# Attention with adaLN and a mixer MLP on one core: wq resident in wo's place, K and V loaded in one stretch, one TensorE-transposed tile a head

## The chip, the cores and the metric

The kernel runs on one core of one Trainium2 chip. The metric is the device time of one execution in microseconds, as the median of the runs.

## The reference

All tensors are bf16; S = 2048 rows, D = 640, 32 heads of 128, 2048 keys a head.

```
mod = (silu(c) @ w_mod) -> sa, ca, ga, sb, cb, gb          # six vectors of 640
h = layernorm(x) * (1 + ca) + sa
q = h @ wq                       # wq: 640 x 4096, 128 columns for each head
p = softmax(q k^T / sqrt(128))   # k, v come from the caches: 32 x 2048 x 128 each
x = x + ga * ((p v, heads side by side) @ wo)               # wo: 4096 x 640
h = layernorm(x) * (1 + cb) + sb
x = x + gb * B(h)                # layernorm, w1, gelu, shifted rows, w2, residual,
                                 # layernorm, w3, gelu, w4, residual
```

## The kernel before

The program is written with a small helper that records every operation with the keys that it reads and writes, derives the waits, and issues each engine's operations in the order in which they were recorded. TensorE (PE), VectorE (DVE), ScalarE (ACT), GpSimd (POOL) and SyncE (SP) each run their own list in order. All DMAs but the ones that write the attention output are on SP's queue, `q1` in the profile; those are on GpSimd's.

There are three stages. At the start x, the modulation weights, the first heads' wq, K and V and then all of wo are loaded, x is normalized and laid out as `hT`, and head 0's Q is made. The second and longest stage is attention; the third applies wo and the MLP.

Attention walks over 512 steps `s`, 16 query tiles of 128 rows for each of 32 heads (`h, j = divmod(s, 16)`). The work for one tile:

- **QK** (line 286, TensorE): four matmuls into `Sps`, two halves of 1024 keys. It needs K of the head, transposed, in one of two buffers of `KTs`, and Q of the head in `QT`.
- **Scale and minimum** (line 559, DVE): for each half, from `Sps` into one of three buffers of `negS`, with the running minimum. POOL joins the two minima (line 569).
- **Exponential** (line 572, ACT): from `negS` into one of the eight slots of `Pb` (`ring`, `RPB = 8`).
- **Transpose of P**: into one of twelve slots of `PTs` (`RPT = 12`). Most tiles go by a DMA transpose on SP's queue (line 222), two tiles of the same pair in one issue where both are free. A tile in `PE_TILES` goes over TensorE instead: in two halves `r`, at steps `s - 3` and `s - 4`, eight 128 x 128 transposes each into one of two PSUM banks (`Oaug`, `QPp`), and each half is copied out, by ACT (line 262) or, for the second half of tile 3, by DVE (line 264).
- **P·V** (line 299, TensorE): sixteen matmuls, 11 steps behind the exponential (8 at the end); ACT copies pairs of outputs to `Of` (line 550); POOL normalizes four tiles into `On` (line 447) and writes them to a scratch tensor in HBM (line 454).

Beside this, Q of the next head is made in pieces of one matmul (line 237), twenty for each head, in the same two PSUM banks, in the half steps that the transposes leave free (`taken`, `QPIECE`), and ACT copies it out (line 244).

Loads for later heads stand in the same loop, on SP's queue between the transposes, so their place in the loop is their place in the queue: K of the next head after tile 2 (`load_k`, line 205), wq of the head after the next after tile 6 (`load_wq`, line 209, 640 rows of 256 bytes), V of the next head after tile 12 (`load_v`, line 214). The `wo` tile, 40 KB in each partition, is filled once at the start (line 335) and read only in the third stage (line 631); later w3, w4 and the output buffers lie in its place.

Of the kernel before, what the change touches and what calls it, by code (L numbers as in the profile page):

```python
# [115 lines left out]
def bass_adaLN_cond__mha_block_cached__mixer_s_mlp__prompt_kernel(  # L116
# [3 lines left out]
    _, H, SK, DH = A_k_cache.shape  # L120
    FF = B_w3.shape[1]
    assert DH == 128 and D % 128 == 0 and SQ % 512 == 0 and SK == 2048
    KT = D // 128
    NQT = SQ // 128
    NQC = SQ // 512
    NKT = SK // 128
    NFT = (FF + 127) // 128
    FL = FF - (NFT - 1) * 128
# [9 lines left out]
    with ExitStack() as es:  # L138
# [11 lines left out]
        if True:  # L150
            with ExitStack() as es1:
                sb1 = lambda name, shape, dt: es1.enter_context(nc.sbuf_tensor(name, shape, dt))
                RPB, RPT = 8, 12
                PVD, PVE = 11, 8
                PE_TILES = (3, 10)
                US = KT * (SQ + 4)
                sb1("pad", [128, 32], F32)
                ring = sb1("ring", [128, RPB + RPT, SK], BF16)
# [14 lines left out]
                o3 = o2 + 2 * KT * 128  # L173
                KTs = kv[:, 0:o1].rearrange("p (b s) -> p b s", b=2)
                Vaug = kv[:, o1:o2].rearrange("p (b k d) -> p b k d", b=2, k=NKT)
                wq = kv[:, o2:o3].rearrange("p (b k d) -> p b k d", b=2, k=KT)
                QT = kv[:, o3:o3 + 2 * SQ].rearrange("p (b q) -> p b q", b=2)
                Pb = ring[:, 0:RPB]
                PTs = ring[:, RPB:RPB + RPT].rearrange("p r (k q) -> p r k q", k=NKT)
# [23 lines left out]
                def load_k(h):  # L203
                    hb = h % 2
                    G.dma("sync", lambda e: e.dma_start_transpose(KTs[:, hb], A_k_cache[0, h]), ("k", hb), w=[("KT", hb)])

                def load_wq(h):
                    hb = h % 2
                    G.dma("sync", lambda e: e.dma_start(wq[:, hb], A_wq[:, h * 128:(h + 1) * 128].rearrange("(k p) d -> p k d", p=128)),
                          ("wq", hb), w=[("wq", hb)])  # L210

                def load_v(h):
                    hb = h % 2
                    G.dma("sync", lambda e: e.dma_start(Vaug[:, hb, :, 0:128], A_v_cache[0, h].rearrange("(t p) d -> p t d", p=128)),
                          ("v", hb), w=[("V", hb)])
# [16 lines left out]
                    return bank_of[key]  # L232

                def q_piece(h, cc, q):
                    hb = h % 2
                    jb = bank(("q", h, cc))
                    G.op("tensor", lambda t: t.matmul(JB[jb], wq[:, hb, q, :], hT[:, q, cc * 512:(cc + 1) * 512],  # L237
                                                      start=(q == 0), stop=(q == KT - 1)),
                         r=[("wq", hb), ("hT", cc, q)], w=[("J", jb)])

                def q_evac(h, cc):
                    hb = h % 2
# [20 lines left out]
                    else:  # L263
                        G.op("vector", lambda v: v.tensor_copy(dst, src), r=[("J", jb)], w=[("PT", g % RPT, r)])

                by_dve = lambda g, r: r == 1 and g % NQT == PE_TILES[0]

                taken = [u for j in PE_TILES for u in range(2 * (j + 3), 2 * (j + 5))]
                QPIECE = {}
                u = 0  # L270
                for cc in range(NQC):
# [53 lines left out]
                load_mod(0, wmod, 0, 2 * D)  # L325
                for cc in range(2, NQC):
                    load_x(cc)
                load_wq(0)
                load_k(0)
                load_v(0)  # L330
                load_mod(1, wmodr, 2 * D, 6 * D)
                if H > 1:
                    load_wq(1)
                    load_k(1)
                G.dma("sync", lambda e: e.dma_start(wo[:], A_wo.rearrange("(h p) n -> p h n", p=128)), "wo", w=["wo"])

                G.op("gpsimd", lambda g: g.memset(ident[:], 0.0), w=["id0"])
                G.op("gpsimd", lambda g: g.memset(ones_f, 1.0), w=["onesf"])
# [106 lines left out]
                def norm(gr, z):  # L445
# [5 lines left out]
                    if z < 3:  # L451
# [33 lines left out]
                vet = sm[:, 336:336 + 3 * NQT].rearrange("p (l t) -> p l t", l=3)  # L485
                mhalf = sm[:, 384:385]
                NEG = [("negS", i) for i in range(3)]
                KVK = ([("KT", b) for b in range(2)] + [("V", b) for b in range(2)] + [("wq", b) for b in range(2)]
                       + [("QT", b, cc) for b in range(2) for cc in range(NQC)])
                HTK = [("hT", cc, k) for cc in range(NQC) for k in range(KT)]  # L490
                ONK = [("On", b, z) for b in range(2) for z in range(4)]
# [24 lines left out]
                for s in range(at[-1] + LAG + 1):  # L516
# [10 lines left out]
                    for half in range(2):  # L527
                        if s < NG:
                            qk(s, half)
                        for g_ in pvs:  # L530
                            if len(pvs) == 1:
                                pv(g_, half)
                            elif g_ == pvs[half]:
                                pv(g_, 0)
                                pv(g_, 1)
                        if s == 0 and half == 1:
                            q_head0(NQC - 1)
                        if h + 1 < H and 2 * j + half in QPIECE:
                            cc, q = QPIECE[2 * j + half]
                            q_piece(h + 1, cc, q)  # L540
                            if q == KT - 1:
                                evacs.append((q_evac, h + 1, cc))
                        for r in range(2):
                            g = s - 3 - r
                            if 0 <= g < NG and is_pe(g):
                                t_piece(g, r, half)
                                if half == 1:
                                    evacs.append((t_evac, g, r))
# [19 lines left out]
                    if s < NG:  # L568
                        G.op("gpsimd", lambda g, r8=r8: g.tensor_scalar(  # L569
                            out=nm[:, r8:r8 + 1], in0=nm0[:, r8:r8 + 1], scalar1=nm1[:, r8:r8 + 1], scalar2=None, op0=ALU.min),  # L570
                            r=[("nmh", 0, r8), ("nmh", 1, r8)], w=[("nm", r8)])
                        G.op("scalar", lambda a, s=s, r8=r8: a.activation(  # L572
                            Pb[:, s % RPB, :], negS[:, s % 3, :], ACT.Exp, bias=nm[:, r8:r8 + 1], scale=-1.0),
                            r=[("negS", s % 3), ("nm", r8)], w=[("Pb", s % RPB)])
                        if not is_pe(s):
                            if s % 2 == 1 and not is_pe(s - 1):
                                transpose(s - 1, 2)
                            elif s % 2 == 1 or is_pe(s + 1):
                                transpose(s, 1)
                        if j == 2 and h >= 1 and h + 1 < H:  # L580
                            load_k(h + 1)
                        if j == 6 and h + 2 < H:
                            load_wq(h + 2)
                        if j == PVD + 1 and h + 1 < H:
                            load_v(h + 1)
                    for g_ in NORMS.get(s, []):
                        gr, z = divmod(g_, 4)
                        if z == 0:
# [35 lines left out]
                def a_pe(j):  # L624
                    b = ybank()
                    pr, z = divmod(j, 2)

                    def f(t):
                        for c0, cw in NC2:
                            for hh in range(H):  # L630
                                ins = t.matmul(YB[b][:, c0:c0 + cw], OTj[pr % 2][:, 2 * hh + z, :], wo[:, hh, c0:c0 + cw],  # L631
                                               start=(hh == 0), stop=(hh == H - 1))
                        return ins
                    G.op("tensor", f, r=[("OT", pr % 2), "wo"], w=[("S", b)])
                    return b

                def a_s1(j, b):
# [35 lines left out]
                for i in range(NQT + 1):  # L673
# [12 lines left out]
                    if 2 <= i:  # L686
                        nrm_of(1, i - 2)
                w3s = B_w3.rearrange("(k p) n -> p k n", p=128)
                G.dma("sync", lambda e: e.dma_start(w3, w3s), "w3", w=["w3", "wo"])
                G.dma("sync", lambda e: e.dma_start(w4[:, 0:NFT - 1, :], B_w4[0:(NFT - 1) * 128, :].rearrange("(f p) n -> p f n", p=128)),  # L690
                      "w4", w=["w4", "wo"])
                G.dma("sync", lambda e: e.dma_start(w4[0:FL, NFT - 1, :], B_w4[(NFT - 1) * 128:FF, :]), "w4b", w=["w4b", "wo"])
                DEL = [1, -1, 2, -2]
                segs = []
                for n in range(KT):
# [67 lines left out]
                def e_op(j):  # L763
                    b = ybank()
                    g = (j // 4) % 2
                    u = j % 2
                    q0 = (j % 4) * 128

                    def f(t):
                        for c0, cw in NC2:  # L770
                            for f_ in range(NFT):
                                ins = t.matmul(YB[b][:, c0:c0 + cw], gT[g][0:fsz[f_], f_, q0:q0 + 128], w4[0:fsz[f_], f_, c0:c0 + cw],  # L772
                                               start=(f_ == 0), stop=(f_ == NFT - 1))
                        return ins
                    G.op("tensor", f, r=["w4", "w4b", ("gT", g)], w=[("S", b)])
                    G.op("vector", lambda v: v.tensor_add(out=tmp[:, u], in0=YB[b][:, 0:D], in1=xb[:, j]),  # L776
                         r=[("S", b), ("xb", j)], w=[("tmp", u)])
                    G.op("vector", lambda v: v.tensor_mul(out=tmp[:, u], in0=tmp[:, u], in1=mod_bc[:, 3 * D:4 * D]),
                         r=[("tmp", u), "mod"], w=[("tmp", u)])
                    G.op("vector", lambda v: v.tensor_add(out=ob[:, u], in0=tmp[:, u], in1=xt[:, j]),  # L780
                         r=[("tmp", u), ("x1", j)], w=[("ob", u)] + (["wo"] if j < 2 else []))
                    G.dma("sync", lambda e: e.dma_start(out2d[j * 128:(j + 1) * 128, :], ob[:, u]), ("out", u), r=[("ob", u)], w=[("o", j)])

                for n in range(KT):
# [59 lines left out]
```

## Time and profile before

| | us |
|---|---|
| median of 3 runs | 1612.16 (1607.38 to 1612.76) |
| the profiled execution | 1604.1 |
| its span, from the first to the last instruction | 1602.3 |
| first exponential of head 0 starts | 39.1 |
| first exponential of head 1 | 81.0 |
| first exponential of head 31 | 1216.2 |
| last exponential starts | 1251.9 |

How to read the profile: the page gives each engine's busy time in the span, a row of tenths over 40 slices, the DMA queues, the chain that ended last, and the costliest groups of instructions by source line. A group's row has its count, then the busy time in all and the mean ns of one, then the idle time of its engine just before it and what ended that. The table by windows gives for a stretch of the span the busy us of PE, PEld (TensorE's weight loads), DVE, ACT and POOL with their instructions in brackets, then the granted TensorE clock, the share of time of the sixteen DMA engines (packets overlap, so it can be over 1) and GB/s. The view of waits has, for each pair of a waiting line and what it waited for, the us in all, the number of times and the longest.

### The profile page before, as it was taken

How to read it: one execution, taken by the hardware profiler on the slowest of the kernel's cores; microseconds unless marked ns; L12 is line 12 of the kernel's file. 1: busy time of each engine (PE TensorE's matmuls, PEld its weight loads, DVE VectorE, ACT ScalarE, POOL GpSimd, SP SyncE). 2: the span in 40 equal slices, each digit the busy share in tenths (PEclk: the TensorE clock that was granted, in tenths of full speed). 3: DMA queues.
4: the chain of work that ended last, by engine and by line, in shares of the span. 5: the costliest groups of instructions: out<-in, count | busy, mean ns of one | idle time of the engine just before them, and what ended most of it. 6: DMA issues, size and time to landing. Idle time of an engine off the chain costs nothing.

```text
span 1602.3 us, 34804 instructions
## 1 busy us (share of the span) xinstructions
PE 1492.6 (93%) x13978; PEld 963.0 (60%) x14231; DVE 1392.5 (87%) x2460; ACT 1288.2 (80%) x1145; POOL 622.8 (39%) x1394
## 2 busy tenths in 40 slices
PE   5799999999999999999999999999999799999998
PEld 3466666666666666666666666666666555545444
DVE  6999999999999999999999999999999266666424
ACT  4999999999999999999999999999999300055330
POOL 0144444444444444444444444444444423322000
PEclk9999999999999999999999999999999899999999
DMA  9999999999999999999999999999999994530000
GB/s 305 229 230 239 238 243 237 253 241 240 237 237 233 239 237 237 239 239 247 243 250 246 250 239 235 246 228 239 236 244 244 241 196 106 106 111 1 17 17 34
DMA packets 1167730, 333.62 MB, mean 208 GB/s; under 512 B 1148304, under 2 KB 1161552, under 8 KB 1167568
## 3 DMA queue, kind: packets, MB, share of 16 engines
q1 hardware_dynamic: 1161424, 314.59, 98.3%
q0 software_dynamic: 6144, 16.79, 3.3%
q8 instruction: 112, 1.84, 0.5%
q14 instruction: 50, 0.41, 0.1%
HBM read 43.48 MB, written 19.40 MB: 39 GB/s over the span
## 4 chain that ended last, share of the span: by engine, by line
DVE 30%; ACT 24%; PE 20%; DMA 15%; issue 10%; POOL 0%; SPq 0%; ACTq 0%; DVEq 0%
DVE negS L559 27%; ACT ring L572 19%; DMA ring<-ring 13%; PE Sps L631 8%; PE Sps L772 4%; PE Oaug L756 2%; PE QPp L756 2%; ACT ring L262 2%; ACT Of L550 2%; PE Sps L741 1%; ACT kv L244 1%; DMA ring<-in_A_x_dram 1%; DVE ring L364 1%; DMA negS<-o_scratch 1%; PE Sps L286 1%
## 5 line engine op out<-in xcount | busy, mean ns | idle before, releaser
L559 DVE TENSOR_SCALAR_CACHE_REDUCE negS<-Sps 128x1024 f32<-128x1024 f32 x1024 | 1177.2, 1220 | 22.2 <-PE Sps L286 12.5
L572 ACT ACTIVATE ring<-negS,small 128x2048 bf16<-128x2048 f32 x512 | 1011.4, 2029 | 21.9 <-DMA ring<-ring 15.7
L299 PEld LDWEIGHTS PTp<-kv,ring 128*128 128x128 bf16 x8192 | 560.0, 98 | 245.0 <-DMA ring<-ring 6.7
L286 PE MATMUL Sps<-kv 128*128 128x512 bf16 x1949 | 596.3, 383 | 62.8 <-DVE negS L559 42.9
L299 PE MATMUL PTp<-kv,ring 128*128 128x129 bf16 x8192 | 645.6, 221 | 6.5 <-DMA ring<-ring 5.6
L569 POOL TENSOR_SCALAR small<-small 128x1 f32<-128x1 f32 x512 | 145.8, 285 | 621.5 <-DVE negS L559 621.4
L286 PEld LDWEIGHTS Sps<-kv 128*128 128x128 bf16 x2048 | 124.5, 97 | 187.2 <-DVE negS L559 158.0
L447 POOL TENSOR_SCALAR On<-Of,small 128x128 bf16<-128x128 f32 x512 | 189.8, 371 | 13.0
L669 ACT COPY kv<-PTp 128x640 bf16<-128x640 bf16 x32 | 22.0, 692 | 155.0 <-PE PTp L666 154.9
L440 POOL TENSOR_TENSOR small<-Of,small 128x4 f32<-128x4 f32 x128 | 133.2, 1040 | 6.3 <-ACT Of L550 6.2
L454 POOL DMA_DIRECT2D o_scratch<-On x128 | 103.1, 806 | 40.8 <-POOL On L447 37.2
L237 PE MATMUL Oaug<-hTx,kv 128*128 128x512 bf16 x265 | 101.2, 387 | 7.9 <-ACT ring L262 4.2
L550 ACT COPY Of<-PTp 128x259 f32<-128x259 f32 x256 | 99.5, 389 | 10.5 <-PE PTp L299 10.5
L237 PE MATMUL QPp<-hTx,kv 128*128 128x512 bf16 x259 | 97.5, 381 | 2.5 <-ACT hTx L391 1.8
L559 DVE DVE_READ_ACCUMULATOR negS<-Sps 128x1 f32 x1024 | 85.4, 83 | 0.0
L612 POOL TENSOR_SCALAR On<-On 128x1 f32<-128x1 f32 x48 | 24.3, 507 | 152.9 <-DVE On L621 152.9
L639 DVE TENSOR_TENSOR ring<-Sps,mod_bc 128x640 f32<-128x640 f32 x16 | 13.2, 825 | 77.0 <-PE Sps L631 77.0
L631 PE MATMUL Sps<-wo,hTx 128*128 128x128 bf16 (+1 forms) x504 | 71.8, 304 | 5.0 <-DMA hTx<-o_scratch 4.7
L776 DVE TENSOR_TENSOR ring<-Sps,ring 128x640 f32<-128x640 f32 x16 | 13.2, 825 | 66.2 <-PE Sps L772 66.2
L631 PE MATMUL Sps<-wo,negS 128*128 128x128 bf16 (+1 forms) x504 | 69.1, 298 | 1.3 <-DMA negS<-o_scratch 0.9
L262 ACT COPY ring<-Oaug 128x1024 bf16<-128x1024 bf16 x64 | 66.2, 1034 | 0.0
L631 PEld LDWEIGHTS Sps<-wo,hTx 128*128 128x128 bf16 x512 | 40.2, 99 | 36.9 <-DMA hTx<-o_scratch 4.5
(82 smaller groups left out, 1011.2 us busy)
## 6 DMA issues: line engine op xcount, KB each, us to landing
kv<-in_A_v_cache_dram SPq DMA_DIRECT2D x32, 512.0 KB, 5.2
o_scratch<-On POOLq DMA_DIRECT2D x128, 128.0 KB, 4.5
ring<-in_A_x_dram SPq DMA_DIRECT2D x8, 640.0 KB, 4.9
kv<-in_A_wq_dram SPq DMA_DIRECT2D x32, 160.0 KB, 3.6
wo<-in_A_wo_dram SPq DMA_DIRECT2D x1, 5120.0 KB, 16.4
ring<-ring SPq DMA_TRANSPOSE x256, 7.1
ring<-in_w_mod_dram SPq DMA_DIRECT2D x1, 3200.0 KB, 13.6
out_dram<-wo SPq DMA_DIRECT2D x16, 160.0 KB, 1.8
```

The costliest lines, as they stand in the source:

```text
L237: G.op("tensor", lambda t: t.matmul(JB[jb], wq[:, hb, q, :], hT[:, q, cc * 512:(cc + 1) * 512], start=(q == 0), stop=(q == KT - 1)), r=[(" ...
L262: G.op("scalar", lambda a: a.copy(dst, src), r=[("J", jb)], w=[("PT", g % RPT, r)])
L286: ins = t.matmul(Sps[:, col:col + 512], QT[:, hb, j * 128:(j + 1) * 128], KTs[:, hb, col:col + 512], start=True, stop=True)
L299: ins = t.matmul(ob[:, 0:129], PTs[:, b, kt, :], Vaug[:, hb, kt, 0:129], start=(kt == 0), stop=(kt == NKT - 1))
L440: G.op("gpsimd", lambda g: g.tensor_tensor(out=rl[:, 4 * b:4 * b + 4], in0=Of[:].rearrange("p a z d -> p (a z) d")[:, 4 * b:4 * b + 4, 128 ...
L447: G.op("gpsimd", lambda g: g.tensor_scalar(out=On[:, b, z, :], in0=Of[:, 2 * b + z // 2, z % 2, 0:128], scalar1=rl[:, 4 * b + z:4 * b + z ...
L454: G.dma("gpsimd", lambda e: e.dma_start(o_scr[jj // 2:jj // 2 + 2, :, hh].rearrange("a p z d -> p a (z d)"), On[:, b].rearrange("p (a z) d ...
L550: G.op("scalar", lambda a, p=p: a.copy(Of[:, p % 4].rearrange("p z d -> p (z d)")[:, 0:259], PO[:, (p % 2) * 512:(p % 2) * 512 + 259]), r= ...
L559: G.op("vector", lambda v, half=half, s=s, r8=r8: v.tensor_scalar(out=negS[:, s % 3, half * 1024:(half + 1) * 1024], in0=Sps[:, half * 102 ...
L569: G.op("gpsimd", lambda g, r8=r8: g.tensor_scalar(out=nm[:, r8:r8 + 1], in0=nm0[:, r8:r8 + 1], scalar1=nm1[:, r8:r8 + 1], scalar2=None, op ...
L572: G.op("scalar", lambda a, s=s, r8=r8: a.activation(Pb[:, s % RPB, :], negS[:, s % 3, :], ACT.Exp, bias=nm[:, r8:r8 + 1], scale=-1.0), r=[ ...
L631: ins = t.matmul(YB[b][:, c0:c0 + cw], OTj[pr % 2][:, 2 * hh + z, :], wo[:, hh, c0:c0 + cw], start=(hh == 0), stop=(hh == H - 1))
```

## The change

- `wq` is no longer loaded head by head into two buffers. It lies whole in the `wo` tile, in eight groups of four heads (`WG = 4`, view `wqg`), all loaded at the start: head 0, then heads 1 to 3, then seven groups of four, 640 rows of 1024 bytes each.
- `wo` is loaded in eight blocks of four heads (512 rows of 1280 bytes), each when the Q of its four heads has been made: after tile 11 of heads 3, 7, ..., 31.
- K and V of the next head are loaded together after tile 11, in this order, followed in every fourth head by the block of wo. V had its place one tile later, K nine tiles earlier.
- `PE_TILES` is tile 11 alone, with a lag of four steps instead of three: its halves are transposed at steps 15 and 16, the second one within the next head. Both are copied out by ACT. Tiles 3 and 10 go by DMA: 3 in a pair with 2, 10 alone.
- Q's pieces move to the half steps 2 to 21 of a head.

```diff
-                PE_TILES = (3, 10)
+                PE_TILES = (11,)
+                PE_LAG = {10: 3, 11: 4}
+                WG = 4
...
-                wq = kv[:, o2:o3].rearrange("p (b k d) -> p b k d", b=2, k=KT)
+                wqg = wo[:].rearrange("p (g h) n -> p g (h n)", h=WG).rearrange("p g (k c) -> p g k c", k=KT)
...
-                def load_wq(h):
-                    hb = h % 2
-                    G.dma("sync", lambda e: e.dma_start(wq[:, hb], A_wq[:, h * 128:(h + 1) * 128].rearrange("(k p) d -> p k d", p=128)),
-                          ("wq", hb), w=[("wq", hb)])
+                def load_wq(h0, h1):
+                    g, c0 = divmod(h0, WG)
+                    G.dma("sync", lambda e: e.dma_start(
+                        wqg[:, g, :, c0 * 128:(c0 + h1 - h0) * 128],
+                        A_wq[:, h0 * 128:h1 * 128].rearrange("(k p) d -> p k d", p=128)),
+                        ("wq", h0), w=[("wq", h) for h in range(h0, h1)])
+
+                def load_wo(g):
+                    G.dma("sync", lambda e: e.dma_start(
+                        wo[:, g * WG:(g + 1) * WG, :],
+                        A_wo[g * WG * 128:(g + 1) * WG * 128, :].rearrange("(h p) n -> p h n", p=128)),
+                        ("wo", g), w=[("wo", g)] + [("wq", h) for h in range(g * WG, (g + 1) * WG)])
...
-                by_dve = lambda g, r: r == 1 and g % NQT == PE_TILES[0]
-
-                taken = [u for j in PE_TILES for u in range(2 * (j + 3), 2 * (j + 5))]
+                by_dve = lambda g, r: False
+
+                taken = [u % (2 * NQT) for j in PE_TILES for u in range(2 * (j + PE_LAG[j]), 2 * (j + PE_LAG[j] + 2))]
...
-                load_wq(0)
+                load_wq(0, 1)
                 load_k(0)
                 load_v(0)
                 load_mod(1, wmodr, 2 * D, 6 * D)
-                if H > 1:
-                    load_wq(1)
-                    load_k(1)
-                G.dma("sync", lambda e: e.dma_start(wo[:], A_wo.rearrange("(h p) n -> p h n", p=128)), "wo", w=["wo"])
+                load_wq(1, WG)
+                load_k(1)
+                for g in range(1, H // WG):
+                    load_wq(g * WG, (g + 1) * WG)
...
-                        for r in range(2):
-                            g = s - 3 - r
-                            if 0 <= g < NG and is_pe(g):
+                        for r, pt in [(r, pt) for r in range(2) for pt in PE_TILES]:
+                            g = s - PE_LAG[pt] - r
+                            if 0 <= g < NG and g % NQT == pt:
                                 t_piece(g, r, half)
...
-                        if j == 2 and h >= 1 and h + 1 < H:
-                            load_k(h + 1)
-                        if j == 6 and h + 2 < H:
-                            load_wq(h + 2)
-                        if j == PVD + 1 and h + 1 < H:
-                            load_v(h + 1)
+                        if j == PVD:
+                            if 1 <= h < H - 1:
+                                load_k(h + 1)
+                            if h < H - 1:
+                                load_v(h + 1)
+                            if h % WG == WG - 1:
+                                load_wo(h // WG)
```

The rest of the diff renames keys: Q's pieces read `wqg`, and what waited for `wo` now waits for its eight blocks.

More of the change, by code (lines that the diff above doesn't have):

```diff
@@ L205, in load_k @@
                     G.dma("sync", lambda e: e.dma_start_transpose(KTs[:, hb], A_k_cache[0, h]), ("k", hb), w=[("KT", hb)])
-                def load_wq(h):
-                    hb = h % 2
-                    G.dma("sync", lambda e: e.dma_start(wq[:, hb], A_wq[:, h * 128:(h + 1) * 128].rearrange("(k p) d -> p k d", p=128)),
-                          ("wq", hb), w=[("wq", hb)])
+                def load_wq(h0, h1):
[9 more added lines that the diff above has]
+                        ("wo", g), w=[("wo", g)] + [("wq", h) for h in range(g * WG, (g + 1) * WG)])
+                WOK = [("wo", g) for g in range(H // WG)]
                 def load_v(h):
@@ L234, in q_piece @@
                 def q_piece(h, cc, q):
-                    hb = h % 2
                     jb = bank(("q", h, cc))
-                    G.op("tensor", lambda t: t.matmul(JB[jb], wq[:, hb, q, :], hT[:, q, cc * 512:(cc + 1) * 512],
+                    G.op("tensor", lambda t: t.matmul(JB[jb], wqg[:, h // WG, q, (h % WG) * 128:(h % WG + 1) * 128], hT[:, q, cc * 512:(cc + 1) * 512],
                                                       start=(q == 0), stop=(q == KT - 1)),
-                         r=[("wq", hb), ("hT", cc, q)], w=[("J", jb)])
+                         r=[("wq", h), ("hT", cc, q)], w=[("J", jb)])
                 def q_evac(h, cc):
@@ L487, in bass_adaLN_cond__mha_block_cached__mixer_s_mlp__prompt_kernel @@
                 NEG = [("negS", i) for i in range(3)]
-                KVK = ([("KT", b) for b in range(2)] + [("V", b) for b in range(2)] + [("wq", b) for b in range(2)]
+                KVK = ([("KT", b) for b in range(2)] + [("V", b) for b in range(2)]
                        + [("QT", b, cc) for b in range(2) for cc in range(NQC)])
@@ L633, in f @@
                         return ins
-                    G.op("tensor", f, r=[("OT", pr % 2), "wo"], w=[("S", b)])
+                    G.op("tensor", f, r=[("OT", pr % 2)] + WOK, w=[("S", b)])
                     return b
@@ L688, in bass_adaLN_cond__mha_block_cached__mixer_s_mlp__prompt_kernel @@
                 w3s = B_w3.rearrange("(k p) n -> p k n", p=128)
-                G.dma("sync", lambda e: e.dma_start(w3, w3s), "w3", w=["w3", "wo"])
+                G.dma("sync", lambda e: e.dma_start(w3, w3s), "w3", w=["w3"] + WOK)
                 G.dma("sync", lambda e: e.dma_start(w4[:, 0:NFT - 1, :], B_w4[0:(NFT - 1) * 128, :].rearrange("(f p) n -> p f n", p=128)),
-                      "w4", w=["w4", "wo"])
-                G.dma("sync", lambda e: e.dma_start(w4[0:FL, NFT - 1, :], B_w4[(NFT - 1) * 128:FF, :]), "w4b", w=["w4b", "wo"])
+                      "w4", w=["w4"] + WOK)
+                G.dma("sync", lambda e: e.dma_start(w4[0:FL, NFT - 1, :], B_w4[(NFT - 1) * 128:FF, :]), "w4b", w=["w4b"] + WOK)
                 DEL = [1, -1, 2, -2]
@@ L780, in e_op @@
                     G.op("vector", lambda v: v.tensor_add(out=ob[:, u], in0=tmp[:, u], in1=xt[:, j]),
-                         r=[("tmp", u), ("x1", j)], w=[("ob", u)] + (["wo"] if j < 2 else []))
+                         r=[("tmp", u), ("x1", j)], w=[("ob", u)] + (WOK if j < 2 else []))
                     G.dma("sync", lambda e: e.dma_start(out2d[j * 128:(j + 1) * 128, :], ob[:, u]), ("out", u), r=[("ob", u)], w=[("o", j)])
```

## The prediction

> **What bounds the kernel now.** I read the page first. Parts 1 and 2 show a softmax stage that fills three quarters of the span, with every engine row and the DMA row at 9 from about 80 to 1250 us; part 3 shows one queue taking nearly all DMA time; part 5 names the two heaviest lines. Nothing there says which of DVE, ACT and DMA is the limit.
>
> ```profile
> PE 1492.6 (93%) x13978; PEld 963.0 (60%) x14231; DVE 1392.5 (87%) x2460; ACT 1288.2 (80%) x1145; POOL 622.8 (39%) x1394
> ...
> DMA  9999999999999999999999999999999994530000
> ...
> q1 hardware_dynamic: 1161424, 314.59, 98.3%
> q8 instruction: 112, 1.84, 0.5%
> ...
> L559 DVE TENSOR_SCALAR_CACHE_REDUCE negS<-Sps 128x1024 f32<-128x1024 f32 x1024 | 1177.2, 1220 | 22.2 <-PE Sps L286 12.5
> L572 ACT ACTIVATE ring<-negS,small 128x2048 bf16<-128x2048 f32 x512 | 1011.4, 2029 | 21.9 <-DMA ring<-ring 15.7
> ```
>
> So I cut the stage into heads (the table by windows). An early head takes 37.2 us, and DVE and ACT are both busy for all of it; a later one takes 37.5 to 39.6, with the same work in it and idle time beside it. The DMA rate is the same in all of them.
>
> ```profile
> 118.30:155.50 37.20, 35.73 (x366) 24.22 (x372) 37.20 (x66) 37.20 (x33) 17.44 (x40) 1.00 1.23 240
> 192.70:229.90 37.20, 35.80 (x368) 24.21 (x372) 37.20 (x66) 37.20 (x32) 17.44 (x40) 1.00 1.25 241
> ...
> 493.20:532.40 39.20, 36.51 (x371) 24.65 (x375) 37.63 (x66) 37.45 (x32) 17.46 (x40) 1.00 1.24 231
> 532.40:571.00 38.60, 35.48 (x364) 24.32 (x369) 36.99 (x66) 37.30 (x32) 17.43 (x40) 1.00 1.23 242
> ```
>
> The waits in 416 to 611 us name what ends the idle time, which the stretch 81 to 378 does not have at all: the exponential waits for a transpose to free its slot in the ring of eight.
>
> ```profile
> PE Sps L286 <- DVE negS L559: 8.5, 20, 1.4
> ACT ring L572 <- DMA ring<-ring: 7.1, 11, 1.2
> ...
> DVE negS L559 <- ACT ring L572: 3.6, 6, 1.5
> ```
>
> To see where that comes from I put the 256 transposes of line 222, in order, beside the exponentials that they need. From the end of the second exponential of tiles 0 and 1 to the landing of their transpose it is 6.2 us in head 0, then 8.9, 9.6, 10.3, 11.6, 12.7, 13.0 in heads 1 to 6, 16.1 in head 12, and 12 to 17 in all heads from 7 to 30. The backlog grows by about 1 us a head while the engines run at 37.2, then stands against the ring's limit. **The DMA queue is the bound from head 1 on**: it needs about 38.0 us a head, and the engines merely run ahead of it by eight tiles. (SyncE's waits are no evidence against it: the view books them under ACT operations, L550 and L244 among them, that no transpose needs.) Between 416 and 611 us packets were under way with next to none starting (a stall) for 29 us, and there was nothing to do for 2 us.
>
> **Prices on the queue.** In a backlogged queue the time from one landing to the next is a service time. Means in 420 to 1200 us, per head: a pair of tiles 3.52 us with no instruction fetch and no write of On in it; a single tile 1.95 to 2.08; K 2.24; V 2.72; wq 0.96 (0.81 without fetches); the pair behind wq 3.93, which is 0.41 more than the plain pair; a write of On adds about 0.9 to the pair that it meets. Each 16 KB packet of q8 is followed by a stall of 0.8 to 1.9 us; PE's instructions (13978 + 14231, 64 bytes each, make 1.81 MB of the 1.84) cause them, 2.9 a head. All twelve intervals of a head add up to 38.0.
>
> **The change, part by part, for one head.**
>
> Removed from DVE: the copy L264. From ACT: one of three L262.
>
> ```profile
> L264 DVE COPY ring<-QPp 128x1024 bf16<-128x1024 bf16 x8 | 5.5, 685 | 0.0
> ```
>
> From its start to the next start the DVE copy is 0.60 us, an ACT copy 0.90 (neighbours overlap by 0.08 and 0.13). DVE then needs 37.22 - 0.60 = 36.62, ACT 37.22 - 0.90 = 36.32. Neither is worth anything while DMA needs more. TensorE loses 16 of its 32 transposes, about 1 us at 8 in 0.8 us; it waits for DVE (L286 above), so that is worth nothing.
>
> Added to DMA: tile 3 and tile 10 join, tile 11 leaves, so 15 tiles instead of 14, still in eight issues (seven pairs and a single for six pairs and two singles). A tile is half of 3.52, +1.76; a single that becomes a pair gives 3.52 - 2.0 = +1.5, a lone single +2.0. I take 1.76, as the tile is moved by the same packets at the same rate as in a pair.
>
> wq leaves the stage: -0.81, and the -0.41 behind it, together -1.2 (ends -0.6, the median interval alone, and -1.4). It is loaded whole at the start in place of wo, 5.24 MB for 5.24 MB, in front of the first transposes as before: nothing. wo comes in eight blocks: at the start all of it took 14.35 us, from K's landing at 32.87 to its own at 47.22; a block is 1.79, per head +0.45 (up to 0.6 with an entry of its own). It is needed only in the next stage; the last block comes in head 31, which loads no K and V.
>
> PE's program shrinks from 744 to 712 instructions a head: 0.125 fetches fewer at some 1.4 us, -0.17.
>
> K and V side by side: the count of switches between transposes and copies around V is the same, and the pair behind V costs no more than one behind a transpose when each holds a write of On (4.27 against 4.44). I put 0.
>
> Sum: 1.76 - 1.2 + 0.45 - 0.17 = **+0.84 us a head, 38.85**. Ends: 1.5 - 1.4 + 0.45 - 0.25 = +0.3 and 2.0 - 0.6 + 0.6 = +2.0. DVE's 36.62 stays below all of these.
>
> The Trainium skill, VectorE: DVE Perf Modes, Rules for kernel authors, speaks against this part: transpose 128×128 on TensorE if PSUM will do as the destination, else by DMA. Advanced Engine Details and Errata, X-Bar Transpose, speaks for it: 350 to 400 GB/s expected, some 90% of a copy. The pair's 1.05 MB in 3.52 us are 298 GB/s here; at the Trainium skill's rate a tile would be an estimated 1.31 to 1.50, and the sum +0.4 to +0.6.
>
> **The moved wait.** K of the next head was issued at tile 2, with fourteen tiles to spare. Now it stands behind the transpose of tile 10 and is needed at tile 16. In the trace the first QK of the next head starts 7.6 us after the exponential of tile 10 ends (6.1 to 7.9 over the heads). K's service is 2.2 us, so the transposes may lag by 5.4 us at most, where 12 are usual. QK is behind the wait, and on TensorE behind it P·V and the second half of tile 11's transposes; DVE runs dry. Since the queue goes on working meanwhile (V, tiles 12/13 and 14/15: 2.7 + 4.3 + 3.8 = 10.8 us, before tiles 0/1 are ready about 8 to 9 us after K lands) the stall is not added to 38.85; it is how the queue's time now shows. What is lost is the head start: tiles 0/1 of the last head will lag by some 7.2 us (10.8 + 4.5 of their own, less 8) where they lagged by 12.9, so the engines end 5.7 us later against the same queue; head 31, free of K and V, gives back 1.8 (33.8 us from its second exponential to its last, against fourteen tiles at 36.62/16).
>
> **Total.** 31 heads x 0.84 = 26, + 5.7 - 1.8 = +30 on the profiled execution: 1604.1 (span 1602.3) becomes 1634. The tail behind the last head is untouched. The median of the runs stands 8 above the profiled time, so **1642**. With the two ends: +13 and +66.
>
> **The rivals.**
>
> *The queue is relieved, not loaded* (faster). If the small wq reads with 256-byte rows cost the transposes around them more than their own interval, or if a tile more in the stream costs less than half a pair, the queue may need less than DVE. For it: 29 us of stalls in 195 are not bytes, and something may be saved there. Against it: the stalls follow the fetches, which stay, and pairs without fetches run evenly at 3.5. Below 36.62 DVE decides: heads 1 to 31 start at 80.4 + 30 x 36.62 = 1179 instead of 1216, and head 31 gains 1: -38, a median of 1574. It is faster than before from -0.13 a head (31 x 0.13 = 3.9), which needs 1 us a head that I have not found. 0.21, most of it between 1580 and 1607.
>
> The Trainium skill, DMA: Bandwidth & Descriptors, Specifications, asks for 512 bytes a transfer for line rate, a rule for this rival. wq's 0.16 MB in 0.81 us are 202 GB/s against wo's 365, so the trace agrees, and that is in the -1.2.
>
> *K's wait starves the queue.* An empty queue takes about 2 us to start (head 0's pairs land 5.5 to 6.0 after the exponential, for a service of 3.5), and 10.8 of work against 8 to 9 plus 2 is a margin of nothing. If the queue stands idle for 1 us at each head, another 31: a median of 1673. For it: QK cannot start without K, and no buffer is left in between. Against it: in most heads a fetch or a write of On stretches those 10.8. 0.15.
>
> *Nothing measurable.* +0.0 a head leaves +4. 0.05.
>
> **How the numbers follow.** The forecast, slower on the queue, 0.59; its own range is 1620 to 1664. What a measurement of this kernel can tell is about 0.3%, 5 us. Faster 0.21, same 0.05, slower 0.59 + 0.15 = 0.74. The range goes from 1592, which leaves out about 0.12 of the faster rival's mass, to 1680, which leaves out 0.06.
>
> **What would show it.** Heads of 38.5 to 39.3 us; DVE at 36.6 busy in each; no copy at L264's place; 15 tiles' packets on q1. At each head's start TensorE and DVE idle together for 1 to 3 us, ended by the DMA kv<-in_A_k_cache_dram, and the exponential's waits for ring<-ring gone; transposes lag by 5 to 9 us, not 14. A lag that stays at 4 to 6 with heads of 36.6 would make the prediction wrong and the first rival right; idle slots in the DMA row at each head's start would mean the second.

## The result and the profile after

The changed kernel takes 1697.03 us (median of 4 runs, 1688.76 to 1702.4) against 1612.46; the ratio is 1.0525, with a 95% interval of 1.0475 to 1.0576. It is slower by about 85 us, where the forecast was slower by 30, and it lies above the stated range.

The page of the kernel after, with the lines that answer to those of before: a DMA row that is still at 9 through the stage, less work on DVE and ACT, more on q1.

```profile
PE 1505.5 (89%) x13474; PEld 968.5 (57%) x13719; DVE 1376.4 (81%) x2428; ACT 1282.6 (76%) x1113; POOL 622.8 (37%) x1394
...
DMA  9999999999999999999999999999999995620000
...
q1 hardware_dynamic: 1211984, 331.36, 97.7%
...
L570 DVE TENSOR_SCALAR_CACHE_REDUCE negS<-Sps 128x1024 f32<-128x1024 f32 x1024 | 1177.8, 1220 | 132.2 <-PE Sps L297 129.9
L583 ACT ACTIVATE ring<-negS,small 128x2048 bf16<-128x2048 f32 x512 | 1021.2, 2005 | 37.5 <-POOL small L580 35.0
L297 PE MATMUL Sps<-kv 128*128 128x512 bf16 x1962 | 611.9, 391 | 148.8 <-DMA kv<-in_A_k_cache_dram 101.1
```

The last row holds the news: QK (line 297 now) sat 101 us waiting for K. Before, most of its idle time was ended by DVE, as its row there says:

```profile
L286 PE MATMUL Sps<-kv 128*128 128x512 bf16 x1949 | 596.3, 383 | 62.8 <-DVE negS L559 42.9
```

The DVE row of the kernel after shows 130 us passed on, and the exponential's idle time is no longer ended by the ring.

The table by windows, heads 11 to 14 of the kernel after: DVE works for 36.3 to 37.2 us in each, but a head lasts 37.9 to 44.3. The clock column moves too: it falls with the length of the head.

```profile
487.30:525.20 37.90, 35.77 (x355) 24.20 (x361) 37.23 (x65) 37.00 (x31) 17.72 (x41) 1.00 1.17 245
525.20:569.50 44.30, 35.75 (x350) 24.25 (x354) 36.28 (x65) 36.88 (x31) 17.11 (x40) 0.92 1.22 229
569.50:609.50 40.00, 36.80 (x350) 25.06 (x356) 36.85 (x65) 37.24 (x32) 17.76 (x41) 0.96 1.20 245
609.50:647.60 38.10, 35.17 (x351) 23.88 (x357) 36.73 (x65) 37.07 (x31) 17.10 (x40) 1.00 1.20 238
```

One head's boundary in order of time. A QK pair takes 0.60 us in the first row; the next head's first QK starts 4.57 us after TensorE's last work, when K lands, and takes 1.04; DVE stands idle behind it, and behind DVE the exponential.

```profile
678.15 0.60 PE L297 MATMUL Sps<-kv 128*128 128x512 bf16 x2
...
685.16 1.04 PE L297 MATMUL Sps<-kv 128*128 128x512 bf16 x2 [4.57 <-DMA kv<-in_A_k_cache_dram]
...
686.24 1.23 DVE L570 TENSOR_SCALAR_CACHE_REDUCE negS<-Sps 128x1024 f32<-128x1024 f32 x1 [4.71 <-PE Sps L297]
```

From the start of head 1 to that of head 31 a head takes 37.84 us before and 40.97 after (1135.2 and 1229.2 us over 30).

### The profile page after: what moved, and what is told of

The parts are those of the page before. It is cut to its first block, busy times and chain, and to the rows that moved or that the text cites. A ratio compares the mean times of both kernels' runs of the same rounds, so it can differ in the third digit from the quotient of the medians.

```text
span 1697.2 us, 33782 instructions
## 1 busy us (share of the span) xinstructions
PE 1505.5 (89%) x13474; PEld 968.5 (57%) x13719; DVE 1376.4 (81%) x2428; ACT 1282.6 (76%) x1113; POOL 622.8 (37%) x1394
## 4 chain that ended last, share of the span: by engine, by line
DVE 48%; PE 24%; DMA 11%; issue 8%; ACT 7%; SPq 2%; POOL 1%; POOLq 0%
DVE negS L570 47%; DMA kv<-in_A_k_cache_dram 8%; PE Sps L643 7%; ACT ring L583 5%; PE Sps L784 4%; PE Sps L297 3%; PE PTp L310 2%; PE Oaug L768 2%; PE QPp L768 2%; SPq L234 2%; PE Sps L753 1%; PE QPp L264 1%; DMA ring<-in_A_x_dram 1%; DVE ring L375 1%; DMA negS<-o_scratch 1%
## 5 line engine op out<-in xcount | busy, mean ns | idle before, releaser
L570 DVE TENSOR_SCALAR_CACHE_REDUCE negS<-Sps 128x1024 f32<-128x1024 f32 x1024 | 1177.8, 1220 | 132.2 <-PE Sps L297 129.9
L297 PE MATMUL Sps<-kv 128*128 128x512 bf16 x1962 | 611.9, 391 | 148.8 <-DMA kv<-in_A_k_cache_dram 101.1
L310 PEld LDWEIGHTS PTp<-kv,ring 128*128 128x128 bf16 x8192 | 574.3, 100 | 256.5 <-issue 22.5
L310 PE MATMUL PTp<-kv,ring 128*128 128x129 bf16 x8192 | 661.3, 224 | 6.0 <-DMA ring<-ring 4.7
L297 PEld LDWEIGHTS Sps<-kv 128*128 128x128 bf16 x2048 | 146.3, 99 | 274.9 <-DVE negS L570 131.7
L561 ACT COPY Of<-PTp 128x259 f32<-128x259 f32 x256 | 92.3, 360 | 95.1 <-PE PTp L310 95.0
L465 POOL DMA_DIRECT2D o_scratch<-On x128 | 103.1, 806 | 40.8 <-POOL On L458 37.2
L248 PE MATMUL Oaug<-hTx,wo 128*128 128x512 bf16 x258 | 98.0, 385 | 2.9 <-DVE hTx L407 2.9
L248 PE MATMUL QPp<-hTx,wo 128*128 128x512 bf16 x260 | 98.1, 382 | 2.8 <-ACT hTx L402 2.3
L643 PEld LDWEIGHTS Sps<-wo,hTx 128*128 128x128 bf16 x512 | 40.0, 99 | 37.2 <-DMA hTx<-o_scratch 5.4
L643 PEld LDWEIGHTS Sps<-wo,negS 128*128 128x128 bf16 x512 | 39.5, 98 | 30.9 <-DMA negS<-o_scratch 0.6
```

Source lines behind the costliest of these rows:

```text
L248: G.op("tensor", lambda t: t.matmul(JB[jb], wqg[:, h // WG, q, (h % WG) * 128:(h % WG + 1) * 128], hT[:, q, cc * 512:(cc + 1) * 512], star ...
L297: ins = t.matmul(Sps[:, col:col + 512], QT[:, hb, j * 128:(j + 1) * 128], KTs[:, hb, col:col + 512], start=True, stop=True)
L310: ins = t.matmul(ob[:, 0:129], PTs[:, b, kt, :], Vaug[:, hb, kt, 0:129], start=(kt == 0), stop=(kt == NKT - 1))
L465: G.dma("gpsimd", lambda e: e.dma_start(o_scr[jj // 2:jj // 2 + 2, :, hh].rearrange("a p z d -> p a (z d)"), On[:, b].rearrange("p (a z) d ...
L561: G.op("scalar", lambda a, p=p: a.copy(Of[:, p % 4].rearrange("p z d -> p (z d)")[:, 0:259], PO[:, (p % 2) * 512:(p % 2) * 512 + 259]), r= ...
L570: G.op("vector", lambda v, half=half, s=s, r8=r8: v.tensor_scalar(out=negS[:, s % 3, half * 1024:(half + 1) * 1024], in0=Sps[:, half * 102 ...
```

## The experiments

Theory A: K's late place costs the time. Theory B: the queue is loaded more than the sum said, and K's wait is where it shows. The ratios are against the kernel before; a stretch named heads 1 to 30 goes from the first exponential of head 1 to that of head 31.

**k_back and k_late: K's place, undone and done alone.**

```diff
 # k_back, from the kernel after
-                        if j == PVD:
-                            if 1 <= h < H - 1:
-                                load_k(h + 1)
+                        if j == 2 and 1 <= h < H - 1:
+                            load_k(h + 1)
...
 # k_late, from the kernel before
-                        if j == 2 and h >= 1 and h + 1 < H:
-                            load_k(h + 1)
...
-                        if j == PVD + 1 and h + 1 < H:
+                        if j == PVD and h >= 1 and h + 1 < H:
+                            load_k(h + 1)
+                        if j == PVD and h + 1 < H:
                             load_v(h + 1)
```

> The changed kernel with one thing undone: K of the next head is again issued after tile 2 (V and the blocks of wo stay after tile 11). Theory A (K's late place starves the queue and lets TensorE's clock fall): the 101 us that QK waited for K vanish, the granted clock is 0.99 again, heads take the queue's own 38.9 us, and the time is about 1642 us (1620 to 1660), as the sum of the prediction had it without the wait. Theory B (the fifteenth tile and the blocks of wo load the queue far more than was summed, K's wait only shows it): heads stay at 40 to 41 us, limited by the ring of eight, time 1675 or more.

Measured: 1682.96 us, ratio 1.041 (1.0381 to 1.0439). QK's wait for K is gone, the clock is 0.989, and most of the lost time is still lost. In the waits of its heads 1 to 30 another line has taken K's place, the one that bounded the kernel before:

```profile
ACT ring L583 <- DMA ring<-ring: 108.2, 76, 5.6
DVE negS L570 <- ACT ring L583: 85.2, 74, 5.0
```

Heads take 40.30 us. From head 2 on the transposes lag by 11 to 22 us, 15 in the median, which is again the ring's limit. So theory B holds for most of the loss: the queue needs 40.3 us a head, not 38.85.

> The kernel before with one thing done: K and V of the next head are issued together after tile 11; wq by head, wo whole, tiles 3 and 10 on TensorE as before. Theory A: QK waits for K at each head, 2 to 3 us in the mean, with the clock falling in some; heads of 39.5 to 41 us, time 1655 to 1700. Theory B: the queue needs its 38.0 us as before and the wait replaces the ring's; time 1610 to 1630.

Measured: 1666.98 us, ratio 1.0307 (1.0276 to 1.0339), heads of 39.93 us, QK waiting for K 66 us in 29 waits, lags of mostly 6 to 9 us. Theory A is right too: with the queue's old load, K's place (and V's, one tile earlier) costs 50 us. Here the queue runs dry: over heads 1 to 30 no packet of q1 was under way for 2.33 us a head, against 1.01 in the kernel before, and half of this time lies ahead of the transpose of tiles 4 and 5. That is 1.3 of the 2.1 us by which a head is longer; how much of the rest is TensorE's clock, granted at half for 68 us in this run, was not tested. The two costs do not add (1.041 and 1.0307 alone, 1.0525 together): the kernel after waits for K and no longer for the ring. On top of the fuller queue K's place costs 1.0525 - 1.041, some 18 us, or 14 by the two medians.

**tile11 and t11_skip: the fifteenth tile.** tile11 is the kernel before with `PE_TILES = (11,)`, its lag and both copies by ACT, and nothing else. t11_skip is tile11 with the transpose of tile 3 left out from head 1 on.

```diff
 # t11_skip, from tile11
+                            if j == 3 and h >= 1:
+                                transpose(s - 1, 1)
-                            if s % 2 == 1 and not is_pe(s - 1):
+                            elif s % 2 == 1 and not is_pe(s - 1):
                                 transpose(s - 1, 2)
```

> The kernel before with one thing done: TensorE transposes tile 11 alone, all others go by DMA; K after tile 2, wq by head after tile 6, V after tile 12. By the prediction's prices +1.5 to +2.0 us a head on the queue, less 0.17 for fetches: heads of 39.4 to 39.8, time 1655 to 1670. Theory B (a tile costs the queue more than its pair's half): 1680 or more. Were DVE and ACT the bound, 0.6 us a head less: 1592.

Measured: 1680.48 us, ratio 1.0385 (1.0352 to 1.0419), heads of 40.31 us. Its wait is the ring's:

```profile
ACT ring L573 <- DMA ring<-ring: 102.9, 94, 3.8
```

> The kernel with tile 11 alone on TensorE (K after tile 2, wq by head), with the DMA transpose of tile 3 left out from head 1 on, so that 14 tiles are moved as before the change; P V of that tile works on old data. If a tile costs the queue about 2.4 us when it is backlogged: heads of 37.9, time about 1606. If a tile costs 1.76 and the rest of the 64 us comes from TensorE's new schedule or from ACT's copies: 1625 or more.

Measured: 1611.2 us, ratio 0.998 (0.9954 to 1.0006), heads of 38.13. One tile less on the queue takes back 69 us: 1680.5 - 1611.2 over 31 heads is 2.2 us a tile. It lies between the two figures of the expectation, 2.4 and 1.76, nearer to the first. All the rest of that edit (TensorE's 16 transposes fewer, DVE's copy, ACT's copy, the new half steps) is worth -0.2%, within the interval of nothing.

**wq_resident, wo_left_out, wo_by_8: the weights.** wq_resident is the kernel after with the old tiles on TensorE, K after tile 2, V and the blocks of wo after tile 12.

> The kernel before with one thing done: wq lies in wo's place and wo follows in eight blocks; K after tile 2, V after tile 12, tiles 3 and 10 on TensorE. By the prediction's prices the queue needs 38.0 - 1.2 + 0.45 = 37.25 us a head, which is where DVE and ACT stand (37.22): about 18 us faster, 1594. If the small wq reads cost no more than their median interval of 0.59, the queue needs 37.9 and the time is 1609. Theory B, with blocks of wo that cost more than 1.8 us each: 1612 or more.

Measured: 1615.19 us, ratio 0.999 (0.9968 to 1.0012): nothing.

```diff
 # wo_left_out, from wq_resident
-                        if j == PVD + 1 and h % WG == WG - 1:
+                        if j == PVD + 1 and h == H - 1:
                             load_wo(h // WG)
```

> The kernel before with wq resident in wo's place and only the last block of wo loaded (heads 0 to 27 are then multiplied with what lies there, the columns of wq); K after tile 2, V after tile 12, tiles 3 and 10 on TensorE. If the blocks are what uses up the gain of the wq loads: the queue needs 38.0 - 0.85 = 37.2 us a head and meets DVE and ACT at 37.2; about 18 us below wq_resident, 1597. If the wq loads had been free: 1612 to 1616.

Measured: 1592.72 us, ratio 0.9845 (0.9803 to 0.9887), heads of 37.36. Taking wq's loads out is worth the expected time, and seven blocks of wo eat it: 0.999 - 0.9845 is 23 us, 3.3 us a block. That is a lower bound, since wo_left_out is no longer held by the queue: its exponentials wait for the ring 4.0 us in the whole run, against 24.0 in wq_resident. The landings of wq_resident agree, with 3.6 us a block in the mean of seven. In the packets of a block the first and the last are some 4.2 us apart in most blocks (1.7 at best, in the kernel after), with the rate rising and falling between them. In all eight blocks of wq_resident the first packets of the next transpose start before the block's last, so the price is not a wait of the next entry for that last packet; what it is made of was not separated.

> The kernel before with wq resident in wo's place and wo following in four blocks of eight heads (1.31 MB) instead of eight of four; K after tile 2, V after tile 12, tiles 3 and 10 on TensorE. If a block's price is a fixed part (its packets start and end staggered over the sixteen engines, and the next transpose waits for the last) plus 1.8 us per four heads at the start's rate: a block of eight takes 5.3 instead of twice 3.5, about 7 us less in all, 1605 to 1610 against 1615. If it is paid by the byte at half the start's rate: 7 us each, 1615.

Measured: 1614.92 us, ratio 0.9981 (0.9957 to 1.0005). The landing interval of a block of eight heads was 4.5 us in the mean (three blocks), as if the price were mostly fixed; the time is that of wq_resident (0.9981 against 0.999), and a gain of 7 us is about what the two intervals could still hide. Whether the price is fixed or goes by the byte stays open.

**k_back_skip2: the same program with room on the queue.**

```diff
 # from k_back
+                            if j == 3 and h >= 1:
+                                pass
-                            if s % 2 == 1 and not is_pe(s - 1):
+                            elif s % 2 == 1 and not is_pe(s - 1):
                                 transpose(s - 1, 2)
```

> The changed kernel with K after tile 2 again, and the DMA transposes of tiles 2 and 3 left out from head 1 on (13 tiles a head; P V of these works on old data). Queue theory: with room on the queue DVE is the bound at 36.6 us a head, lags fall to 4 to 8 us, time about 1576 to 1582. If something else than the queue held the heads at 40.3, more than 1600.

Measured: 1566.87 us, ratio 0.9702 (0.9673 to 0.9732). The table by windows over heads 1 to 30 of k_back and of this kernel: DVE, third of the engines, is busy for all of the second, 36.64 us a head, as summed. The time is below the 1576 to 1582 expected, and the transposes lag by 8 to 13 us where 4 to 8 was expected.

```profile
80.80:1289.90 1209.10, 1072.73 (x10500) 706.26 (x10694) 1110.50 (x1923) 1095.50 (x901) 523.85 (x1202) 0.99 1.21 238
```
```profile
80.80:1179.90 1099.10, 1061.48 (x10492) 697.64 (x10685) 1099.10 (x1921) 1092.90 (x901) 523.24 (x1200) 1.00 1.21 234
```

The change does make DVE faster; the queue keeps it from showing.

**warm: TensorE kept busy while it waits for K.** In the kernel after, the granted clock fell to half at 19 of the 30 boundaries, in TensorE's idle time or just behind it, for 3.4 or 6.8 us and once for 10.2. These are the 18 boundaries with 2.8 us of idle time and more, and one with 2.0; at the eleven others, of 1.0 to 2.3, the clock stayed. It is 102 us in all, 25 of them in the idle time itself. In k_late it fell at every boundary with 2.4 us and more, and at six of the eight with 2.0 to 2.3. The Trainium skill, TensorE: Matmul & The Clock Gate, What's actually happening, says that the clock is halved after an idle window of about 3.4 us; the traces agree in the lengths of 3.4 us and its multiples, and show shorter idle times that did it.

```diff
 # from the kernel after
+                        if half == 0 and j == 0 and 2 <= h < H:
+                            warm()   # 28 x matmul(PO[:, 262:512], ident, hT[:, 0, 0:250])
                         if s < NG:
                             qk(s, half)
```

> The changed kernel, with 28 extra matmuls (250 columns each, into unused PSUM columns, result not used) on TensorE ahead of the first QK of heads 2 to 31, about 3 us of work in the time in which TensorE waits for K. Clock theory: in the changed kernel the heads whose wait is over 2.5 us lose another 1 to 2 us because TensorE runs at half clock after it; with the idle time filled, the clock is 0.99, heads that waited briefly lose about 1 us, the others gain; time 1670 to 1690 against 1697, and half clock under 30 us instead of 102. Rival (the clock costs nothing, the queue sets the head in any case): 1697 to 1710.

Measured: 1702.63 us, ratio 1.0526 (1.0478 to 1.0574). Half clock fell to 27 us and TensorE's idle wait for K to 48, but DVE's wait for QK is about what it was in the kernel after (129.9 us):

```profile
DVE negS L579 <- PE Sps L297: 136.2, 44, 7.4
```

The rival's figure was met. About 16 us of delay that the filler adds in the eleven short waits (3.15 us a head in its row, against 1.7 in the mean) may hide a gain of that size, so the clock's own cost is not shown to be nothing; by this working some 16 of the 85 us lost can be the clock's. The queue pauses less in this run, too: no packet of q1 was under way for 1.00 us a head, against 1.54 in the kernel after and 1.06 in k_back, and yet a head takes 41.12 us.

**third_tile and third_tile_by_2: the other way.**

```diff
 # from the kernel before
-                PE_TILES = (3, 10)
+                PE_TILES = (2, 4, 11)
-                is_pe = lambda g: g % NQT in PE_TILES
+                is_pe = lambda g: g % NQT in (2, 11) or (g % NQT == 4 and (g // NQT) % 3 == 1)
-                by_dve = lambda g, r: r == 1 and g % NQT == PE_TILES[0]
+                by_dve = lambda g, r: r == 1 and g % NQT < 11
```

> The kernel before with more on TensorE instead of less: tiles 2 and 11 in every head, and tile 4 in every third head (second halves of 2 and 4 copied by DVE). The queue gives up a third of a tile a head, 2.4 / 3 = 0.8 us, from 38.0 to 37.2; ACT rises by 0.3 to 37.5, DVE by 0.2 to 37.4. If the queue is the bound of the kernel before: heads of 37.5, about 10 to 15 us faster, 1600 to 1606. If DVE and ACT bound it: 1620 to 1625.

Measured: 1602.01 us, ratio 0.9915 (0.9887 to 0.9943), heads of 37.73.

> As third_tile, with tile 4 on TensorE in every second head: the queue gives up 1.1 us a head, ACT rises by 0.45 to 37.67 and DVE by 0.3 to 37.52. ACT is then the bound: heads of 37.7, no better than third_tile, 1600 to 1606; lags of the transposes fall to 6 to 10 us. If the queue still bound third_tile: 1592 or less.

Measured (`% 2` in place of `% 3`): 1599.76 us, ratio 0.9888 (0.9857 to 0.9919), heads of 37.67. Both beat both kernels. The second's exponentials wait for the ring 2.5 us in the whole run, where before it was 15.7. DVE and ACT are both busy for 37.6 of the 37.67 us of a head, so they are the bound now, though the lags, at 9 to 15 us, stayed longer than expected.

```profile
ACT ring L572 <- DMA ring<-ring: 2.5, 3, 1.0
```

The Trainium skill, VectorE: DVE Perf Modes, Rules for kernel authors, which the prediction cited against the change, agrees with these two runs: more tiles on TensorE gave 0.9915 and 0.9888.

## Why the prediction was right and wrong

Right: the bound (the DMA queue, read from lags that grow), that DVE's and ACT's savings would not show, DVE's 36.6 us beneath it, the wait that would appear at the heads' starts and the line that ends it (3.4 us in the mean and up to 7.2, where 1 to 3 was forecast), shorter lags (6.5 to 12.8 us at tile 10, mostly 7 to 10, where 5 to 9 was forecast), and the sign. One reading of its first paragraph is wrong and changes nothing: the rows of PEld and POOL stand at 6 and 4 in the stage, not at 9.

Wrong: the size. Two steps failed. The queue's new entries were priced by rows in which nothing disturbs them, half a quiet pair for the tile and a share of one long transfer for wo's blocks; and the wait for K was put at nothing beyond a lost head start, because the queue was said to go on working meanwhile. The 55 us between 1642 and 1697 come from these terms:

- **The tile, +1.76 in the sum: 2.2 measured**, 15 us over 31 heads. The row was chosen wrongly. Half of an undisturbed pair was taken; a tile's mean in the same trace, fetches and writes of On included, is (27.61 + 4.63) / 13.9 = 2.3 us, and a tile more costs nearly that. The stated end of 2.0 excluded it. What makes up the difference was not separated: the 2048 packets a head that tile11 has over t11_skip, at the some 1050 a microsecond that run between stalls, are an estimated 1.95 us, and the remaining 0.2 to 0.3 is open.
- **wq and wo, -0.75 together: 0 measured**, 22 us. wo's block was priced at the rate of one long transfer at the start (1.8 us) and costs at least 3.3 in the stage; its end of 0.6 a head was too low as well. wq's loads were worth at least 25 us (wo_left_out then meets DVE and ACT), so their -1.2 is neither shown nor refuted beyond 0.8.
- **The moved wait, +3.9 in all: some 18 measured**, 15 us (10 by the medians). "The stall is not added" was the step that failed; with the queue's old load, in k_late, the stall cost 50 us and the queue ran dry. In the kernel after, no packet of q1 was under way for 1.54 us a head, against 1.06 in k_back, most of the difference ahead of tiles 0 and 1, and a head is 0.67 longer. So the rival of the starved queue, which was priced at 1 us a head and given 0.15, happened in addition to the forecast, at half its price by the idle time. It is not shown to be the whole of the 0.67: in warm the queue pauses no more than in k_back and a head is no shorter, and what else adds to it stays open. The prediction also missed that a block of wo makes the next head's K late: TensorE's idle time before the first QK is 5.2 us in the mean after heads 4, 8, ..., 28, whose queue starts behind a block, and 2.8 after the others.
- **Fetches, -0.17 a head**: the whole of TensorE's part is -0.2% in t11_skip, 3 of the 5 us.

15 + 22 + 15 + 2 is 54. That the terms meet the gap so well is in part luck, as each was measured in a kernel of its own and costs of this kind need not add. A ladder that adds up by its making goes from the kernel before over t11_skip (0.998), tile11 (1.0385) and k_back (1.041) to the kernel after (1.0525): what TensorE, DVE and ACT are spared, then the tile, then the weights with V's place, then K's place. In it the weights cost 4 us instead of nothing, within the intervals. The first rival, a relieved queue, has no support as a whole: the tile, wo's blocks and the moved wait came out dearer than summed, and only the absence of wq's loads was worth at least 0.8 us a head. The clock was not foreseen; warm leaves room for some 16 us of it in the loss, and does not show that it cost anything.

The weighed rule of 350 to 400 GB/s (the Trainium skill, Advanced Engine Details and Errata, X-Bar Transpose) is further from these runs than the row was: 0.524 MB in 2.2 us are 238 GB/s.

## What to carry to other kernels

When every engine looks busy, put the landing of each transfer beside the moment at which its data was ready: a lag that grows from loop to loop names the queue as the bound, and its growth is the excess. Price a further entry in a full queue by the mean of its kind in the stage, disturbances included, not by the quietest row: here the mean was 2.3 us a tile, half the quiet pair 1.76, and 2.2 was measured. A load that is moved later in an in-order queue must meet its reader with the lag of the full queue. A wait at a loop's head can take the place of a wait at a full ring, so two such costs are not simply added: here some 50 and 66 us alone were 85 together.

## What the runs showed of the hardware that was not expected

- A plain copy of 0.655 MB between transposes held the queue for at least 3.3 us (by the difference of two kernels) and some 3.6 (by landings), where as many bytes of one long transfer took 1.79.
- TensorE's clock was granted at half for 3.4 or 6.8 us, once 10.2, around idle times from 2.4 us up and some from 2.0, a QK pair taking up to 1.04 instead of 0.60 us; with the idle time filled the half clock fell from 102 to 27 us, and the time stayed at a ratio of 1.053.
